# A hash-attention kernel with two gated layers: normalized rows scaled in place before their transposition, and a copy of the queries moved to a DMA

## The chip, the cores and the metric

The kernel runs on one core of one Trainium2 chip. The metric is device time in microseconds (us) of one execution; lower is better. The time of a kernel is the median of its timed runs.

## The reference, cut to what matters

The attention is masked by hash buckets: a query sees a key only where the signs of six projections agree. Its output is normalized row by row (root mean square) and goes through a gated layer and a layer with a squared ReLU. All numbers are float32.

```python
# attention: batch 2, heads 8, seq 768, head_dim 64
q_bits = (np.einsum('bhsd,dk->bhsk', q, proj) > 0)      # and k_bits
q_bucket = np.sum(q_bits * powers, axis=-1)             # and k_bucket
mask = q_bucket[:, :, :, None] == k_bucket[:, :, None, :]
scores = np.where(mask, scale * np.matmul(q, k.transpose(0, 1, 3, 2)), -1e9)
attn = softmax(scores); x = attn @ v                    # -> [1536 tokens, 512]
# first layer, d_ff 1536
rms = np.sqrt(np.mean(x * x, axis=-1, keepdims=True) + 1e-06)
xn = x / rms * rms_g
g = xn @ w_gate; val = xn @ w_val
x = (g * (1.0 / (1.0 + np.exp(-g))) * val) @ w_out
# second layer, d_ff 2048
r = np.maximum(x @ w_in, 0.0)
out = (r * r) @ w_out
```

## The kernel before, in words

The whole program is a list of small operations. Each has a function that issues its instructions, a rank, a cost for each engine that may run it (T is TensorE, D VectorE, A ScalarE, P GpSimd, S SyncE's queue), what it reads and writes (`r`, `w`) and which buffers it makes or uses (`new`, `use`). At build time `Plan.run` walks over this list: again and again it takes the operation that can start first by those costs, lower rank first among equals, and gives it to the engine where it starts first. The engines' instructions stand in that order; on the chip each engine runs its own in order, and semaphores hold what isn't ready. A change of one cost, one reader or one engine can so move everything that is planned after it.

**Attention.** There are 16 heads, in two batches of 8, with 6 row tiles each: 96 slots. To keep float32 precision, operands are split into a high and a low part. For each head `plan_prep` loads keys (`rk`) and queries (`rq`), splits the keys into `k1` (high part, twice) and `k2` (low part), and the queries into `q1` (high part in partitions 0 to 63, low part in 64 to 127). `copy_q` writes the high part of the queries a second time, into `q2[0:64]`, from `rq`; the hash bits come into the rows of `q2` below (`hash_pe`, `hash_bits`), and 12 rows of them go by a DMA from ScalarE's queue into `k2` (`hash_dma`). The scores of a slot (`st_S`) are matmuls of `q1` with `k1` and of `q2` with `k2`. `k1`, `k2`, `q1` and `q2` have three buffers each, so a new head's copies wait for the last scores of the head three before.

A slot then goes through `st_min` (VectorE, out of PSUM, with the row maximum), `st_exp` (ScalarE), the split of the probabilities into halves of 16 bits, their transposition and the product with the values (`st_PV`). Slots of one kind transpose on TensorE (`st_TP`, L592, 128x128 transposes by an identity); the others split on ScalarE and GpSimd into `hla`, and SyncE's queue issues a DMA transpose into `Ta` (`st_T`, L585). The same queue issues the loads of the values and of all layer weights (`wraw`, L937). At a head's end `st_evac` scales the result into `xall`, which holds 6 tiles of 128 tokens x 512: the 768 tokens of one batch.

**Norm.** When the eight heads of a batch are done, `plan_norm` runs for each half of `xall` (3 tiles, 384 tokens), so four times in all. ScalarE squares and sums each tile (L834), GpSimd takes a power, VectorE improves it by four Newton steps on 128x3 elements (L851 to L859), which gives `rr`, one factor for each row. `scales` makes three diagonal matrices `diag` of 128x128, identity times `rr`. `x_pe` transposes and scales at once: for each of 4 column blocks, three float32 matmuls of an `xall` block with `diag`. `x_hi` and `x_lo` split the result, times `rms_g`, into the operands `xT` of the layers.

**Layers.** Weights arrive as float64 and are turned into two float32 parts by VectorE and ScalarE (L950 to L979). Products of the first batch's tokens are put in between the second batch's attention; the second batch's follow.

Of the kernel before, what the change touches and what calls it, by code (L numbers as in the profile page):

```python
# [10 lines left out]
F32 = mybir.dt.float32  # L11
# [5 lines left out]
AF = mybir.ActivationFunctionType  # L17
ALU = mybir.AluOpType
# [3 lines left out]
B, H, S, D = 2, 8, 768, 64  # L22
# [8 lines left out]
TT = TB // 128  # L31
# [19 lines left out]
OPS = {'k1': 3, 'q1': 3, 'k2': 3, 'q2': 3}  # L51
# [15 lines left out]
R_QC = -12.8  # L67
# [5 lines left out]
R_S = -4.0  # L73
# [11 lines left out]
R_X = 41.4  # L85
# [16 lines left out]
H_K = 2.7  # L102
# [3 lines left out]
KQ = 'A'  # L106
WQ = 'S'
VQ = 'S'


class Op:
# [130 lines left out]
def tile_hash_attention_moe(  # L242
# [44 lines left out]
    rr = const.tile([128, QT], F32, name="rr")  # L287
    rt = const.tile([128, QT], F32, name="rt")
    idle = const.tile([128, 512], F16, name="idle")
    diag = const.tile([128, TT, 128], F32, name="diag")  # L290

    plan = Plan(dict(
        OPS, **RING, rk=RAW, rq=RAW, vr=2, vl=3, O=1, mo=3, mt=MB[0], mu=MB[1], y=YB, yL=YL,
# [5 lines left out]
    def f32(x):  # L299
        return x.bitcast(F32)  # L300

    def copy(eng, out_, in_):
        if eng == "A":
            nc.scalar.copy(out_, in_)  # L304
        elif eng == "D":
            nc.vector.tensor_copy(out_, in_)
        else:
            nc.gpsimd.tensor_scalar(  # L308
                out=out_, in0=in_, scalar1=1.0, scalar2=0.0, op0=ALU.mult, op1=ALU.add
            )  # L310
# [13 lines left out]
    def dma(name, cost):  # L324

        return {"dma": cost, name: 0.475 if name == "S" else 0.1}
# [53 lines left out]
    def tile_of(h, name, n=3, dtype=F32R):  # L380
        t = heads[h][name] = ap.tile([128, S], dtype, tag=name, name=name, bufs=n)
        return t
# [21 lines left out]
        sub(eng, d["q1"][64:128, c], d["rq"][0:64, c], f32(d["q1"][0:64, c]))  # L404

    def copy_q(eng, h):
        copy(eng, tile_of(h, "q2", OPS["q2"])[0:64], heads[h]["rq"][0:64])

    def s_ring(n):

        return "Sb" if n % 2 and n < XEND else "Sa"
# [126 lines left out]
    def st_S(eng, i):  # L538
        h, t = divmod(i, QT)
        d = heads[h]  # L540
        sp = tiles[i]["sp"] = scores(s_ring(i))
        for n, (a, b2, kr) in enumerate((("q1", "k1", 128), ("q2", "k2", RQ + 2 * NB))):
            for hf in range(2):
                nc.tensor.matmul(  # L544
                    sp[:, hf, 0:TB],
                    d[a][0:kr, t * 128:(t + 1) * 128],
                    d[b2][0:kr, hf * TB:(hf + 1) * TB],
                    start=(n == 0), stop=(n == 1),
                )
# [101 lines left out]
    def plan_prep(h):  # L651
# [14 lines left out]
            D=(0.47, H_K), A=0.733, P=0.8,  # L666
        )
        add(
            lambda e: copy_q(e, h), s0 + R_QC, use=[("rq", h)], new=[("q2", ("q2", h))],
            D=(0.47, H_K), A=0.733, P=0.8,  # L670
        )
        for n, c in enumerate((slice(0, TB), slice(TB, S)) if h == 0 else (slice(0, S),)):
            f = 0.55 if h == 0 else 1.0
# [73 lines left out]
    def plan_slot(i):  # L747
# [2 lines left out]
        space = ["more"] if c == "x" else []  # L750
        ko = [(x, h) for x in ("k1", "q1", "k2", "q2")]
        add(
            lambda e: st_S(e, i), i + R_S, use=ko, r=[("head", h)] + [("bits", 0, 1, 0)] * (h == 0 and t >= TT), new=[(s_ring(i), ("S", i))],
            chain="S", T=0.72, w=[("S", i)],
        )
        if i < W1:
# [103 lines left out]

    def scales(eng, hf, t):

        nc.vector.tensor_scalar(
            out=diag[:, t, :], in0=ident, scalar1=rr[:, hf * TT + t:hf * TT + t + 1],
            scalar2=None, op0=ALU.mult,
        )

    def x_pe(eng, st, blk, c):

        pt = st["p"] = mo()[:, 0:TB]  # L870
        for t in range(TT):
            nc.tensor.matmul(
                pt[:, t * 128:(t + 1) * 128],
                xall[:, blk % 2 * TT + t, c * 128:(c + 1) * 128], diag[:, t, :],
                start=True, stop=True,
            )

    def x_hi(eng, st, blk, c):
# [8 lines left out]
    def plan_norm(blk):  # L887
        hf = blk % 2
        for t in range(TT):
            b = ("junk x", blk, t)  # L890
            add(
                lambda e, t=t: squares(e, hf * TT + t), R_X, r=[("x", hf)], w=[("ss", hf, t)],
                new=[("wv", b)], A=0.65,
            )
        sq = [("ss", hf, t) for t in range(TT)]
        add(lambda e: power(e, hf, 0), R_X, r=sq, w=sq + [("rr", hf)], D=0.07)
        add(lambda e: power(e, hf, 1), R_X, r=sq, w=[("rr", hf)], P=0.9)
        for n in range(4):
            add(lambda e, n=n: newton(e, hf, n), R_X, r=[("rr", hf)], w=[("rr", hf)], D=0.08)
        for t in range(TT):  # L900
            add(
                lambda e, t=t: scales(e, hf, t), R_X, r=[("rr", hf), "ident"], w=[("diag", t)],
                D=0.2,
            )
        tag, p = xt_place[1, blk]
        for c in range(4):
            st, b = {}, ("xp", blk, c)
            add(
                lambda e, st=st, c=c: x_pe(e, st, blk, c), R_X + c, new=[("mo", b)], T=0.65,
                r=[("x", hf)] + [("diag", t) for t in range(TT)],  # L910
            )
            add(
                lambda e, st=st, c=c: x_hi(e, st, blk, c), R_X + c, r=[p, b] + [("xt", blk)] * (c > 0),
                use=[b], new=[("xT" + tag, ("xT", 1, blk))] * (c == 0), A=0.464,
                w=[("xh", 1, blk, c)] + [("xt", blk)] * (c == 0),
            )
            add(
                lambda e, st=st, c=c: x_lo(e, st, blk, c), R_X + c, r=[("xh", 1, blk, c)],
                use=[b, ("xT", 1, blk)], w=[("xT", 1, blk, c)], D=0.53,
            )  # L920
# [408 lines left out]
```

## Time and profile before

| | |
|---|---|
| median of 3 runs | 845.27 us (840.51 to 851.2) |
| the profiled execution | 842.59 us, span 840.8 us |
| PE (TensorE matmul) busy | 789.9 us, 94% of the span |
| DVE (VectorE) busy | 711.3 us, 85% |
| ACT (ScalarE) busy | 460.6 us, 55% |
| POOL (GpSimd) busy | 235.2 us, 28% |

The profile is one execution. The span is the time from the first to the last instruction; the execution's own time is 1.8 us longer. PE counts matmuls and PEld the loads of their stationary operand. SPq and ACTq are the queues in which SyncE and ScalarE issue DMAs. A float32 matmul is recorded as two matmuls, a transpose as one.

### The profile page before, as it was taken

What the parts mean: (1) busy time and instruction counts of PE and PEld (TensorE: products, weight loads), DVE (VectorE), ACT (ScalarE), POOL (GpSimd) and SP (SyncE); (2) the same over time, 40 slices, a digit from 0 to 9 for tenths busy, and PEclk for the clock granted to TensorE, in tenths of its full rate; (3) what the DMA queues carried; (4) which work ended last, traced back from release to release, by engine and by line L of the source; (5) the groups of instructions that cost most, each with busy time, mean ns of one, the idle gap of its engine ahead of it and who ended that gap; (6) DMA issues with size and microseconds to landing.
All of it is one profiled execution on the core that took longest, in us unless ns stands there. A gap on an engine that the chain in (4) does not pass through costs nothing.

```text
span 840.8 us, 14918 instructions
## 1 busy us (share of the span) xinstructions
PE 789.9 (94%) x5633; PEld 718.3 (85%) x5633; DVE 711.3 (85%) x1391; ACT 460.6 (55%) x929; POOL 235.2 (28%) x205
## 2 busy tenths in 40 slices
PE   8989896989879998889899999999999999999998
PEld 4777775889768897889789999999899898998996
DVE  6997888789795998889999999999687787877764
ACT  5888897777777787523355334346552342342320
POOL 7578785656666454000001000000000000000000
PEclk8999998999998999999999999999999999999999
DMA  6465766488976998233334343432320211211003
GB/s 225 124 111 115 150 140 163 99 177 206 194 164 122 193 179 167 79 101 101 101 103 149 101 138 130 133 125 75 104 100 26 76 60 41 101 51 51 26 1 150
DMA packets 126528, 97.74 MB, mean 116 GB/s; under 512 B 106308, under 2 KB 108356, under 8 KB 126456
## 3 DMA queue, kind: packets, MB, share of 16 engines
q1 hardware_dynamic: 122960, 87.97, 40.8%
q10 hardware_dynamic: 3496, 8.81, 3.7%
q8 instruction: 44, 0.72, 0.3%
q14 instruction: 28, 0.23, 0.1%
HBM read 67.12 MB, written 3.15 MB: 84 GB/s over the span
## 4 chain that ended last, share of the span: by engine, by line
PE 67%; DVE 22%; issue 3%; ACT 3%; DMA 3%; POOL 2%; ACTq 0%; SPq 0%; DVEq 0%; POOLq 0%
PE mo L1006 32%; PE mo L1113 16%; PE mo L1102 8%; PE S L544 4%; PE O L618 4%; DVE Pa L555 3%; PE S L423 3%; DMA Ta<-hla 2%; DVE mo L956 2%; DVE acc L1127 2%; DVE mo L966 1%; DVE yl L313 1%; DVE mo L970 1%; DVE mo L961 1%; DVE wil L313 1%
## 5 line engine op out<-in xcount | busy, mean ns | idle before, releaser
L313 POOL TENSOR_TENSOR hla<-Pa,hla 128x768 f16<-128x768 f32 x66 | 110.7, 1678 | 72.1 <-ACT hla L304 64.7
L1127 DVE TENSOR_TENSOR acc<-acc,mo 128x512 f32<-128x512 f32 (+1 forms) x164 | 100.9, 617 | 23.6 <-PE mo L1113 22.9
L544 PE MATMUL S<-k,q 76*128 76x384 f32 (+1 forms) x384 | 91.3, 365 | 11.9 <-DVE Pa L555 7.8
L1032 ACT ACTIVATE mt<-mo 128x384 f32<-128x384 f32 x64 | 31.3, 489 | 101.1 <-PE mo L1006 97.7
L544 PEld LDWEIGHTS S<-k,q 76*128 76x128 f32 (+1 forms) x384 | 66.4, 195 | 19.9 <-DVE Pa L555 9.6
L1113 PE MATMUL mo<-woh,yl 128*128 128x512 f32 x192 | 75.3, 392 | 0.0
L1113 PE MATMUL mo<-wol,yh 128*128 128x512 f32 x192 | 75.2, 392 | 0.0
L1113 PE MATMUL mo<-woh,yh 128*128 128x512 f32 x192 | 74.7, 389 | 0.0
L555 DVE TENSOR_SCALAR_CACHE_REDUCE Pa<-S 128x768 f32<-128x768 f32 x66 | 62.6, 949 | 12.5 <-PE S L544 8.5
L313 DVE TENSOR_TENSOR yl<-mu,yh 128x384 fp32r<-128x384 f32 x112 | 67.7, 612 | 3.8 <-POOL yh L308 2.6
L308 POOL TENSOR_SCALAR yh<-mu 128x384 fp32r<-128x384 f32 x19 | 9.9, 524 | 218.0 <-PE mo L1113 88.1
L308 POOL TENSOR_SCALAR wih<-wv 128x512 fp32r<-128x512 f32 x15 | 9.4, 627 | 215.1 <-ACT mt L1032 109.7
L1036 DVE TENSOR_TENSOR mu<-mt 128x384 f32<-128x384 f32 x64 | 35.3, 552 | 36.1 <-ACT mt L1032 36.0
L1102 PE MATMUL mo<-yh,woh 128*128 128x384 f32 x192 | 65.1, 339 | 0.5 <-DVE wil L313 0.5
L1102 PE MATMUL mo<-yh,wol 128*128 128x384 f32 x192 | 64.5, 336 | 0.1
L1102 PE MATMUL mo<-yl,woh 128*128 128x384 f32 x192 | 64.4, 335 | 0.0
L573 ACT ACTIVATE Pa<-Pa,b 128x768 f32<-128x768 f32 x66 | 62.1, 943 | 3.2 <-ACT b L564 0.3
L1006 PE MATMUL mo<-xTAh,wih 128*128 128x384 f32 x160 | 55.8, 349 | 5.2 <-DVE acc L1127 2.9
L950 ACT ACTIVATE wv<-wraw 128x512 f32<-128x512 f32 x70 | 46.4, 670 | 25.9 <-DMA wraw<-in_w 25.8
L304 ACT CAST hla<-Pa 128x768 f16<-128x768 f32 x66 | 54.8, 833 | 5.6 <-DVE q L432 2.4
L1006 PE MATMUL mo<-xTAh,wil 128*128 128x384 f32 x160 | 55.1, 345 | 1.2 <-DVE wil L313 1.1
L1006 PE MATMUL mo<-xTBh,wih 128*128 128x384 f32 x160 | 54.3, 339 | 1.2 <-DVE mu L1026 1.2
(166 smaller groups left out, 2350.3 us busy)
## 6 DMA issues: line engine op xcount, KB each, us to landing
wraw<-in_w SPq DMA_DIRECT2D x104, 512.0 KB
rk<-in_k ACTq DMA_DIRECT2D x14, 384.0 KB
vr<-in_v SPq DMA_DIRECT2D x8, 384.0 KB
out<-acc SPq DMA_DIRECT2D x12, 256.0 KB
rq<-in_q ACTq DMA_DIRECT2D x14, 192.0 KB
Ta<-hla SPq DMA_TRANSPOSE x66
rk<-in_k SPq DMA_DIRECT2D x2, 384.0 KB
k<-q ACTq DMA_DIRECT2D x15, 36.0 KB
```

Source lines behind the costliest of these rows:

```text
L304: nc.scalar.copy(out_, in_)
L313: engine[eng].tensor_tensor(out=out_, in0=in0, in1=in1, op=ALU.subtract)
L544: nc.tensor.matmul(sp[:, hf, 0:TB], d[a][0:kr, t * 128:(t + 1) * 128], d[b2][0:kr, hf * TB:(hf + 1) * TB], start=(n == 0), stop=(n == 1),)
L555: nc.vector.tensor_scalar(out=e["P"].rearrange("p (a b) -> p a b", a=2), in0=e["sp"][:, :, 0:TB], scalar1=-1e9 / SCALE, scalar2=None, op0= ...
L573: nc.scalar.activation(e["P"], e["P"], AF.Exp, bias=e["b"], scale=SCALE)
L618: nc.tensor.matmul(d["O"][:, t, 0:w], T[:, a, :], b2[:, c, :], start=(c == 0 and n == 0), stop=(c == QT - 1 and n == 2),)
L950: nc.scalar.activation(t, f32(wst[m]["hi"]), AF.Abs)
L1006: nc.tensor.matmul(ps, a[:, c * 128:(c + 1) * 128], b2[:, c, :], start=(c == 0 and n == 0), stop=(c == 3 and n == 2),)
L1036: nc.vector.tensor_tensor(out=us["u"], in0=st["t"], in1=st["t"], op=ALU.mult)
L1102: nc.tensor.matmul(po, a[:, dc * 128:(dc + 1) * 128], b2, start=(j == 0 and n == 0), stop=(j == len(fs) - 1 and n == 2),)
L1113: nc.tensor.matmul(po, a[:, tt * 128:(tt + 1) * 128], b2, start=(j == 0 and n == 0), stop=(j == len(fs) - 1 and n == 2),)
L1127: nc.vector.tensor_tensor(out=ac, in0=ac, in1=st["p"], op=ALU.add)
```

## The change

`scales` no longer writes diagonal matrices: it multiplies each tile of `xall` in place by its rows' factors, 128x512 elements, on ScalarE or VectorE, whichever the plan finds free first. `x_pe` transposes the scaled tile by the identity, with the instruction that `st_TP` uses; the 128x3x128 buffer `diag` is gone. For all heads but the first, `copy_q` becomes a DMA in SyncE's queue that copies `q1[0:64]` to `q2[0:64]`, so it follows the split of `q1` and no longer reads `rq`; the scores of a head wait for it by a token `qc`. The planner's costs are changed to match.

```diff
+QQ = 'S'
...
-    diag = const.tile([128, TT, 128], F32, name="diag")
...
     def copy_q(eng, h):
-        copy(eng, tile_of(h, "q2", OPS["q2"])[0:64], heads[h]["rq"][0:64])
+        t = tile_of(h, "q2", OPS["q2"])
+        if h == 0:
+            copy(eng, t[0:64], heads[h]["rq"][0:64])
+        else:
+            engine[eng].dma_start(out=f32(t[0:64]), in_=f32(heads[h]["q1"][0:64]))
...
         add(
-            lambda e: copy_q(e, h), s0 + R_QC, use=[("rq", h)], new=[("q2", ("q2", h))],
-            D=(0.47, H_K), A=0.733, P=0.8,
+            lambda e: copy_q(e, h), s0 + R_QC, use=[("rq" if h == 0 else "q1", h)],
+            new=[("q2", ("q2", h))], w=[("qc", h)],
+            **(dict(D=(0.47, H_K), A=0.733, P=0.8) if h == 0 else dma(QQ, 0.6)),
         )
...
-            lambda e: st_S(e, i), i + R_S, use=ko, r=[("head", h)] + [("bits", 0, 1, 0)] * (h == 0 and t >= TT), new=[(s_ring(i), ("S", i))],
+            lambda e: st_S(e, i), i + R_S, use=ko, r=[("head", h), ("qc", h)] + [("bits", 0, 1, 0)] * (h == 0 and t >= TT), new=[(s_ring(i), ("S", i))],
...
     def scales(eng, hf, t):
 
-        nc.vector.tensor_scalar(
-            out=diag[:, t, :], in0=ident, scalar1=rr[:, hf * TT + t:hf * TT + t + 1],
-            scalar2=None, op0=ALU.mult,
-        )
+        t += hf * TT
+        if eng == "A":
+            nc.scalar.activation(xall[:, t, :], xall[:, t, :], AF.Copy, scale=rr[:, t:t + 1])
+        else:
+            nc.vector.tensor_scalar(
+                out=xall[:, t, :], in0=xall[:, t, :], scalar1=rr[:, t:t + 1], scalar2=None,
+                op0=ALU.mult,
+            )
...
         for t in range(TT):
-            nc.tensor.matmul(
+            nc.tensor.transpose(
                 pt[:, t * 128:(t + 1) * 128],
-                xall[:, blk % 2 * TT + t, c * 128:(c + 1) * 128], diag[:, t, :],
-                start=True, stop=True,
+                xall[:, blk % 2 * TT + t, c * 128:(c + 1) * 128], ident,
             )
...
             add(
-                lambda e, t=t: scales(e, hf, t), R_X, r=[("rr", hf), "ident"], w=[("diag", t)],
-                D=0.2,
+                lambda e, t=t: scales(e, hf, t), R_X, r=[("rr", hf)], w=[("xn", hf, t)] + [("x", hf)] * (t == 0),
+                A=0.52, D=0.34, port=True,
             )
...
-                lambda e, st=st, c=c: x_pe(e, st, blk, c), R_X + c, new=[("mo", b)], T=0.65,
-                r=[("x", hf)] + [("diag", t) for t in range(TT)],
+                lambda e, st=st, c=c: x_pe(e, st, blk, c), R_X + c, new=[("mo", b)], T=0.34,
+                r=["ident", ("x", hf)] + [("xn", hf, t) for t in range(TT)],
```

## Rows read from the trace of the kernel before

**Rows 1.** Four stages: from:to, length, busy PE PEld DVE ACT POOL, clock, DMA share, GB/s
```profile
0.00:140.00 140.00, 123.77 (x1355) 98.54 (x1355) 117.97 (x259) 115.10 (x254) 100.59 (x93) 0.96 0.61 143
140.00:330.00 190.00, 170.56 (x1578) 152.72 (x1579) 163.49 (x306) 145.91 (x287) 113.98 (x80) 0.96 0.79 166
330.00:438.00 108.00, 96.60 (x590) 92.46 (x589) 98.75 (x197) 46.35 (x97) 5.51 (x8) 0.98 0.33 100
438.00:840.00 402.00, 399.00 (x2110) 374.59 (x2110) 331.10 (x631) 153.19 (x294) 15.11 (x26) 1.00 0.26 88
```

**Rows 2.** The page's chain that ended last, by engine
```profile
PE 67%; DVE 22%; issue 3%; ACT 3%; DMA 3%; POOL 2%; ACTq 0%; SPq 0%; DVEq 0%; POOLq 0%
```

**Rows 3.** The chain at the norms: start us, us, what
```profile
156.17 0.69 DVE diag L863 x3
...
339.88 2.68 PE mo L872 x24
...
347.78 1.35 PE mo L872 x12
```

**Rows 4.** The timeline at the first and third norm: start, us, engine, line, operation
```profile
145.57 4.33 PE L872 MATMUL mo<-diag,xall 128*128 128x128 f32 x24 [3.94 <-DVE diag L863]
...
336.80 0.67 DVE L863 TENSOR_SCALAR diag<-ident,rr 128x128 f32<-128x128 f32 x3
...
339.71 2.84 PE L872 MATMUL mo<-diag,xall 128*128 128x128 f32 x24
```

**Rows 5.** The chain in the attention: transposes on TensorE, at L592
```profile
48.86 0.69 PE mo L592 x6
```

**Rows 6.** Operations nearest to the new scaling, by line: ns min/median/max
```profile
L863 DVE TENSOR_SCALAR diag<-ident,rr x12: 274/278/287, 145.2 to 346.6; 128x128 f32<-128x128 f32 x12
...
L956 DVE TENSOR_SCALAR wv<-wv x70: 406/420/890, 24.1 to 813.0; 128x512 f32<-128x512 f32 x70
...
L834 ACT ACTIVATE wv<-xall x12: 619/641/662, 138.0 to 341.5; 128x512 f32<-128x512 f32 x12
```

**Rows 7.** Copies and splits of the queries into q1 and q2, by line and engine
```profile
L308 POOL TENSOR_SCALAR q<-rq x17: 825/829/1002, 6.7 to 263.8; 64x768 fp32r<-64x768 f32 x17
L304 ACT CAST q<-rq x15: 814/832/838, 6.6 to 264.9; 64x768 fp32r<-64x768 f32 x15
```

**Rows 8.** The chain where a copy of the queries or a head's hash lies on it
```profile
28.18 0.81 POOL q L308
...
116.19 0.84 ACT q L304
...
181.37 2.19 PE S L423 x8
```

**Rows 9.** The timeline at the prep of the twelfth head
```profile
161.50 0.83 POOL L308 TENSOR_SCALAR q<-rq 64x768 fp32r<-64x768 f32 x1 [1.41 <-PE S L544]
```

**Rows 10.** ScalarE's DMA queue over the whole span: packets, MB, share of 16 engines
```profile
q10 hardware_dynamic: 3496, 8.81, 3.7%
```

**Rows 11.** Issues in SyncE's queue by line: ns min/median/max
```profile
L585 SPq DMA_TRANSPOSE Ta<-hla x66: 1273/1444/3123, 38.5 to 331.3; - x66
...
L388 SPq DMA_DIRECT2D rq<-in_q x2: 471/539/607, 1.6 to 9.2; - x2
```

**Rows 12.** Who waited for whom: total us, times, longest
```profile
SPq L585 <- POOL hla L313: 87.6, 35, 6.8
...
POOL q L308 <- PE S L544: 7.2, 5, 2.1
...
PEld L618 <- DMA Ta<-hla: 5.9, 6, 2.0
```

**Rows 13.** The granted clock in two stretches: columns as in the first group
```profile
64.00:141.00 77.00, 67.84 (x869) 56.81 (x868) 65.87 (x145) 67.13 (x155) 58.90 (x52) 1.00 0.63 136
141.70:148.50 6.80, 2.93 (x13) 2.93 (x14) 5.08 (x14) 4.19 (x13) 4.72 (x3) 0.50 1.08 225
```

**Rows 14.** The chain's longest wait for a DMA transpose
```profile
220.66 7.23 DMA Ta<-hla
```

## The prediction, made before the change was run

> **What bounds the kernel now.** I read the busy time by stage first, then the chain of work that ended last, then the norms and the queries' copies where that chain meets them. Four stages differ [rows 1]. From 438 us to the end TensorE is busy 399.0 of 402 us: nothing outside it counts there, and neither part of the change is in that stretch, so those 402 us stay. The gain or loss must come out of the first 438 us, where TensorE idles 16.2, 19.4 and 11.4 us in the three stages, 47 us in all. There no engine is alone: in the attention VectorE runs at 84 to 86%, ScalarE at 77 to 82%, DMA at 0.61 to 0.79 of its time; from 330 to 438 us VectorE is at 91% and ScalarE and GpSimd have room. The chain [rows 2] says the same: 67% TensorE, 22% VectorE, 3% each for ScalarE and DMA, 2% GpSimd. The last 402 us alone are some 48 of TensorE's 67 points. What is left in the first 438 us, of 840.8 us, is 160 us of TensorE, 185 us of VectorE, and some 25 us each of ScalarE and DMA. So a microsecond of TensorE's taken away there is on the chain about one time in three, one of VectorE's two times in five, and one of ScalarE's or GpSimd's one time in twenty.
>
> **Transposes for matmuls.** Each of the four norms issues 12 float32 matmuls, 24 records, which took 2.84 us at the third norm and 4.33 us at the first [rows 4]. The nearest row of what replaces them is the attention's own transposes: 6 in 0.69 us of the chain [rows 5], 0.115 us each, one record. 12 of them are 1.4 us, half the third norm's time. TensorE is thus spared some 1.4 us at each of three norms and 2.1 us at the first: 6.3 us of its 789.9. On the chain lie 24 records of the third norm and 12 of the fourth, 4.03 us [rows 3]; 18 transposes take 2.07 us. Gain there: 2.0 us. At the first norm TensorE had waited 3.94 us for `diag` [rows 4], and the chain passes beside its matmuls; of the 2.1 us I count 0.5. Bounds of the whole: 0 and 6.3 us.
>
> [...]
>
> **Scaling in place for diagonals.** Removed: three VectorE operations of 0.278 us, 0.68 us a norm [rows 4, 6]. Added: three of 128x512. [...] On ScalarE the nearest is the square of the same tile, 0.64 us [rows 6], 1.9 us a norm. [...] At the third it is covered: `diag` was complete at 337.5 us, TensorE came to it at 339.7 us [rows 4]. Only at the second do the diagonals stand on the chain [rows 3]. I take +0.8 us there, and 0.4 to 4.8 us as bounds over four norms: the new wait is TensorE's for the last tile, with whatever the plan puts behind the transposes, and behind the scaling on ScalarE stand the evacuation and the squares of the other half, so a late factor now holds these too. If ScalarE takes the last two norms' scaling, as its free time after 330 us suggests [rows 1], VectorE, which is the chain there, does 1.3 us less; I take -0.7 us, bounds -1.3 and +0.8.
>
> **The queries' second copy.** 15 copies of 64x768 leave ScalarE and GpSimd, at 0.83 us each [rows 7]: 12.4 us of engine time. The chain shows just two of the 30 copies that `q1` and `q2` need, 0.81 and 0.84 us [rows 8], and doesn't tell which of the two is which. I take -1.6 us; bounds 0 and -12.4, the latter if every copy on GpSimd, which the slots' low parts wait behind, were a delay to its end.
>
> What takes their place: 15 DMAs of 197 KB. ScalarE's queue moved 8.81 MB in 3.7% of 840.8 us of all 16 engines [rows 10], 283 GB/s, so one is 0.69 us of DMA time and all are 10.4 us, into stages whose DMA share is 0.61 to 0.79 [rows 1]. By the chain's share of DMA, 25 of 438 us, that is +0.6 us. SyncE's queue issues each in some 0.54 us [rows 11], 8 us in all, and that queue is 0% of the chain [rows 2]. Its new wait is for the split of `q1`. Behind it stand DMA transposes and the weights' loads, and TensorE's product with the values waits for the former. The copy itself has time: the twelfth head's queries were copied at 161.5 us [rows 9] and its hash came to TensorE at 181.4 us [rows 8]; scores follow still later. Bounds: 0 where every transfer is hidden (a gain is excluded: nothing is taken from these queues), and at the other end the second rival's 23 us.
>
> **The sum.** -2.0 - 0.5 + 0.8 - 0.7 - 1.6 + 0.6 = -3.4 us. The profiled execution is 842.6 us, 1.8 us over its span, so 839.2 us; the median shown is 2.7 us above that execution, which gives 841.9 us. Between the two I forecast 840 us, 0.6% less. A measurement of this kernel tells about 2%, 17 us, from no change: below 828 us is faster, above 862 us slower. Since the plan is dealt anew from the second head on, I give this case 834 to 847 us, a chance of 0.60.
>
> **Rivals.**
> 1. The engines' time pays in full. ScalarE's and GpSimd's 12.4 us and TensorE's 6.3 us are all saved, since a list that takes what can start first fills the holes: 842.6 - 18.7 = 824 us, 833 with half of it. For it: the attention stages have no engine under 60% [rows 1], and SyncE's transposes waited 87.6 us for GpSimd's low parts [rows 12]. Against: ScalarE and GpSimd are 5 points of the chain. Chance 0.16.
> 2. SyncE's queue becomes the place that waits. A copy stands at the queue's head until `q1` is split, which itself waits for the last scores of three heads before; the longest such wait was 2.1 us [rows 12]. With the issue of 0.54 us and 0.69 us of transfer, the transposes behind come 3.3 us late. Transposes run from 38.5 us on [rows 11], so the ten copies after the fifth count: 33 us if each delay reached TensorE, 12 us if a third did, which is 855 us; with two thirds, 23 us, it is 866 us. It decides from the point where a transpose's data is ready before the copy's; the chain already has one wait of 7.2 us for a transpose [rows 14]. Against: TensorE's loads waited for transposes 5.9 us in all of 66 [rows 12]. This ends slower than before. Chance 0.13.
> 3. The clock falls at the norms. The stretch from 141.7 to 148.5 us at 0.50 [rows 13] made the first norm's matmuls 1.5 us longer than the third's. One such stretch of 6.8 us costs at most 3.4 us of work; at three further norms up to 10 us: 840 + 3 to 10 = 843 to 850 us. [...] Chance 0.06.
> 4. The change doesn't reach the end: the copies and the scaling are hidden both before and after, TensorE's holes grow by what its work shrinks, 842 to 846 us. Chance 0.05.
>
> **How the numbers follow.** The range is to leave out no more than 2 in 10. Below it lies the lower part of rival 1, above it the upper part of rival 2, and a remainder near both ends of the first case: 828 to 853 us. Faster by over 2% is about half of rival 1, 0.09. Slower by over 2% is a part of rival 2, 0.05. The rest, 0.86, is no change that can be told.
>
> **What the profile after would show.** L872's place should hold 48 transposes instead of 96 records, some 1.4 us for 12 of them at full clock; no VectorE operation writes `diag`; `xall` has 12 more writers of 0.4 or 0.65 us. ScalarE and GpSimd should have 15 fewer copies of 64x768, SyncE's queue 15 more issues. TensorE should be saturated again from some point on, 2 to 6 us earlier; its busy time there must be the same 399 us. The prediction is wrong if that point moves by over 10 us: earlier by fewer waits of GpSimd's and TensorE's in the attention (rival 1), or later with TensorE's waits for transposes well above 6 us (rival 2) or further stretches at clock 0.50 around the norms (rival 3).

## The result, and the profile after

The changed kernel takes 851.6 us, the median of 20 runs (846.51 to 857.48); the kernel before takes 844.9 us, the median of 20 runs on the same chips. The ratio is 1.0085, with a 95% interval of 1.0067 to 1.0102: 0.85% or 7.2 us slower (the two medians differ by 6.7 us), where 0.6% faster was forecast. The time lies inside the range given and on the other side of no change.

The profiled execution after has a span of 849.0 us, before 840.8 us. The four stages after, with the columns of [rows 1]:

```profile
0.00:140.00 140.00, 124.45 (x1351) 99.08 (x1351) 113.73 (x247) 110.70 (x249) 96.43 (x86) 0.95 0.72 162
140.00:330.00 190.00, 171.30 (x1494) 153.29 (x1495) 163.39 (x301) 134.39 (x262) 107.75 (x83) 0.93 0.75 161
330.00:438.00 108.00, 92.31 (x595) 88.35 (x594) 97.98 (x190) 53.60 (x112) 13.24 (x12) 0.95 0.38 106
438.00:840.00 402.00, 400.85 (x2127) 376.93 (x2126) 335.88 (x644) 156.48 (x300) 15.07 (x26) 1.00 0.26 85
```

The last 402 us are full, as before (399.0 us): the loss lies ahead of 438 us. The second stage is the striking one. TensorE is busy as long as before, 171.3 against 170.6 us, and issues 84 matmuls fewer, 24 of them by the transpositions; the granted clock there is 0.93 and not 0.96. So busy time alone hides the loss. I therefore read busy time times granted clock, which is about what TensorE got done, in us at the clock of 1.00: a transposition took 0.115 us there [rows 5] and 0.23 us at 0.50 (below). The clock's column has two digits, so each product holds to about 1 us. First before, then after, in three stretches:

```profile
161.00:241.00 80.00, 73.51 (x642) 65.92 (x641) 69.55 (x120) 62.39 (x122) 51.69 (x37) 1.00 0.83 179
241.00:330.00 89.00, 81.82 (x791) 73.13 (x790) 76.65 (x147) 69.33 (x136) 50.03 (x33) 0.96 0.80 163
330.00:441.00 111.00, 99.55 (x607) 95.41 (x607) 101.68 (x202) 47.74 (x100) 5.51 (x8) 0.98 0.34 105
```

```profile
161.00:241.00 80.00, 66.56 (x516) 58.67 (x517) 68.98 (x121) 53.89 (x111) 45.39 (x36) 0.87 0.73 164
241.00:330.00 89.00, 87.28 (x829) 80.37 (x829) 79.90 (x147) 64.67 (x122) 49.07 (x37) 1.00 0.81 175
330.00:441.00 111.00, 95.31 (x611) 91.16 (x610) 100.98 (x196) 55.14 (x115) 13.24 (x12) 0.95 0.38 107
```

From 161 to 241 us before does 73.5 x 1.00 = 73.5 us of work and after 66.6 x 0.87 = 57.9: it falls back by 15.6 us in the 80 us that follow the first norm, some 7 of them by idle time and the rest by the lower clock. From 241 to 330 us it wins back 8.7 (87.3 against 78.5), and from 330 to 441 us it loses 7.1 (90.5 against 97.6). That is 14.0 us behind; its own work is some 6 us smaller, by 96 records of 0.118 us [rows 4] for 48 of 0.115 us [rows 5], and the span is 8.2 us longer. Up to 441 us as a whole TensorE idles just 2.8 us more than before; the larger part of what it falls behind is the lower clock (0.94 for 0.97). First before, then after:

```profile
0.00:441.00 441.00, 393.87 (x3540) 346.67 (x3541) 383.14 (x766) 308.75 (x638) 220.09 (x179) 0.97 0.62 144
```

```profile
0.00:441.00 441.00, 391.06 (x3454) 343.53 (x3455) 378.10 (x742) 300.23 (x624) 217.43 (x180) 0.94 0.65 148
```

The change did what it says. After, by line: 48 transpositions for 96 records [rows 3], the scaling on ScalarE eight times and on VectorE four, ns min/median/max:

```profile
L881 PE MATMUL mo<-ident,xall x48: 272/419/477, 144.9 to 362.1; 128*128 128x128 f32 x48
...
L870 ACT ACTIVATE xall<-xall,rr x8: 707/723/733, 144.1 to 359.4; 128x512 f32<-128x512 f32 x8
...
L872 DVE TENSOR_SCALAR xall<-xall,rr x4: 478/487/1739, 145.3 to 359.2; 128x512 f32<-128x512 f32 x4
```

The scaling is dearer than its nearest rows [rows 6]: 0.723 us on ScalarE (0.641 there) and 0.487 on VectorE (0.420), with one of 1.74. Most transpositions of the first two norms ran at the lower clock: it was granted at 0.50 from 144.7 to 151.5 and from 178.9 to 182.3 us. The chain after shows them there (start us, us, what):

```profile
147.07 1.12 PE mo L881 x4
...
149.17 1.33 PE mo L881 x6
...
178.80 2.57 PE mo L881 x11
```

The last is 0.23 us for each; twelve at that pace are 2.8 us, no less than the 24 records that they replace [rows 4]. What TensorE and its loads waited for (total us, times, longest) answers to [rows 12]; the first row is L544 and L555 of before, where it was 7.8 us in 10 waits:

```profile
PE S L548 <- DVE Pa L559: 12.5, 12, 2.8
...
PEld L622 <- DMA Ta<-hla: 3.7, 8, 1.5
```

The waits for the DMA transposes have become fewer, 3.7 for 5.9 us. Those for the row maxima `Pa`, which free the scores' buffers, have grown. TensorE's longest single wait in this kernel is another one, in the stretch that loses 7.1 us:

```profile
411.53 0.69 PE L1014 MATMUL mo<-xTAh,wih 128*128 128x384 f32 x1 [6.08 <-DVE wol L313]
```

VectorE converts weights almost without a gap from 405.6 us on, and TensorE stands until it is through. The same wait, 6.0 to 6.1 us, is in every profile with the changed kernel's order or nearly that (e4, e12, e13, e16 and e17 below). In the other orders TensorE waits at most 4.7 us at a time between 330 and 441 us, in the kernel before 2.9.

### The profile page after: what moved, and what is told of

It reads as the page before. It is cut to its first block, busy times and chain, and to the rows that moved or that the text cites. A ratio compares the mean times of both kernels' runs of the same rounds, so it can differ in the third digit from the quotient of the medians.

```text
span 849.0 us, 14861 instructions
## 1 busy us (share of the span) xinstructions
PE 794.1 (94%) x5585; PEld 721.6 (85%) x5585; DVE 714.2 (84%) x1383; ACT 455.2 (54%) x921; POOL 232.5 (27%) x206
## 4 chain that ended last, share of the span: by engine, by line
PE 72%; DVE 18%; ACT 3%; issue 2%; DMA 2%; POOL 1%; SPq 0%; ACTq 0%; DVEq 0%; POOLq 0%
PE mo L1014 33%; PE mo L1121 16%; PE mo L1110 9%; PE S L548 6%; PE O L622 4%; PE S L427 2%; DMA Ta<-hla 2%; DVE Pa L559 2%; DVE mo L974 1%; PE mo L596 1%; DVE mo L964 1%; DVE yl L313 1%; DVE q L436 1%; POOL hla L313 1%; DVE acc L1135 1%
## 5 line engine op out<-in xcount | busy, mean ns | idle before, releaser
L548 PE MATMUL S<-k,q 76*128 76x384 f32 (+1 forms) x384 | 96.5, 378 | 16.2 <-DVE Pa L559 12.5
L548 PEld LDWEIGHTS S<-k,q 76*128 76x128 f32 (+1 forms) x384 | 68.7, 202 | 24.1 <-DVE Pa L559 15.6
L308 POOL TENSOR_SCALAR yh<-mu 128x384 fp32r<-128x384 f32 x24 | 13.1, 546 | 216.8 <-PE mo L1121 88.1
L313 DVE TENSOR_TENSOR yl<-mu,yh 128x384 fp32r<-128x384 f32 x112 | 65.7, 595 | 6.1 <-POOL yh L308 3.2
L308 POOL TENSOR_SCALAR wih<-wv 128x512 fp32r<-128x512 f32 x12 | 7.5, 624 | 208.1 <-ACT mt L1040 109.7
L1014 PE MATMUL mo<-xTAl,wih 128*128 128x384 f32 x160 | 55.9, 349 | 0.0
```

Source lines behind the costliest of these rows:

```text
L313: engine[eng].tensor_tensor(out=out_, in0=in0, in1=in1, op=ALU.subtract)
L548: nc.tensor.matmul(sp[:, hf, 0:TB], d[a][0:kr, t * 128:(t + 1) * 128], d[b2][0:kr, hf * TB:(hf + 1) * TB], start=(n == 0), stop=(n == 1),)
L1014: nc.tensor.matmul(ps, a[:, c * 128:(c + 1) * 128], b2[:, c, :], start=(c == 0 and n == 0), stop=(c == 3 and n == 2),)
```

## The experiments

Three theories stand in what was expected. A: the plan deals a new order, and this order loses time on TensorE, by holes and by the low clock that follows them. B: the norm's new instructions cost it, the transpositions by holding the clock down. C: the copies in SyncE's queue cost it. All ratios are to the kernel before, run on the same chip; 0.1% is 0.84 us. A new deal also moves operations from engine to engine: the kernel before has 1391 instructions on VectorE, 929 on ScalarE and 205 on GpSimd; in e10, which changes two planning numbers and nothing else, they are 1396, 920 and 209. "Order" stands here for both, and no run takes the two apart.

**The two parts alone, each planned for itself.** e1 has the new norm and the copies of before; e2 has the norm of before and the copies by DMA.

```diff
# e1, on the changed kernel
-            engine[eng].dma_start(out=f32(t[0:64]), in_=f32(heads[h]["q1"][0:64]))
+        copy(eng, tile_of(h, "q2", OPS["q2"])[0:64], heads[h]["rq"][0:64])
# e2, on the kernel before
-        copy(eng, tile_of(h, "q2", OPS["q2"])[0:64], heads[h]["rq"][0:64])
+            engine[eng].dma_start(out=f32(t[0:64]), in_=f32(heads[h]["q1"][0:64]))
```

> Only the norm is changed (scaling in place, transposes); the second copy of the queries stays on the engines; the plan is dealt anew. Theory A (the new order of the plan loses the time, by holes on TensorE and the half clock that follows them): anything from 838 to 856 us, with the time going up by about half of the added microseconds at half clock plus the added idle time of TensorE. Theory B (transposes at the norms hold the clock down): near the changed kernel, 849 to 853 us, with half clock at each norm. Theory C (SyncE's queue and the copies' DMAs cost the time): below the kernel before, 838 to 843 us.

> Only the queries' second copy is changed (a DMA in SyncE's queue); norm with diagonals as before; the plan is dealt anew. Theory A: anything from 838 to 856 us, again told by TensorE's holes and half clock. Theory B: as the kernel before or a little less, 842 to 845 us. Theory C: 850 to 855 us, with TensorE waiting longer for DMA transposes.

e1: 846.1 us, ratio 1.0009 (0.9984 to 1.0034). e2: 839.05 us, 0.9941 (0.9914 to 0.9968), faster than both kernels. One part does nothing, the other gains 0.6%, together they lose 0.85%: the parts don't add, so what each does in an order of its own doesn't explain the whole. C as a cost of the queue by itself falls: with all 15 DMAs in the queue e2 is the fastest kernel of this study.

**The change in the order of before.** In e3 the list of operations with its costs, readers and engines is that of before, so every engine's order stays; only what `scales`, `x_pe` and the copies issue is new. The scaling falls to VectorE, and a head's DMA is issued right behind the split of `q1`. e5 is e3 with ordinary matmuls by the identity, e6 is the norm's half of e3, e7 the copies' half. In e3, e5 and e7 `copy_q` copies for the first head alone.

```diff
# e3; e6: the first two hunks; e7: the third; e5: all, with matmul for transpose
-            out=diag[:, t, :], in0=ident, scalar1=rr[:, hf * TT + t:hf * TT + t + 1],
+            out=xall[:, hf * TT + t, :], in0=xall[:, hf * TT + t, :],
+            scalar1=rr[:, hf * TT + t:hf * TT + t + 1], scalar2=None, op0=ALU.mult,
...
-            nc.tensor.matmul(
+            nc.tensor.transpose(
-                xall[:, blk % 2 * TT + t, c * 128:(c + 1) * 128], diag[:, t, :],
+                xall[:, blk % 2 * TT + t, c * 128:(c + 1) * 128], ident,
...
+        if h > 0:
+            nc.sync.dma_start(
+                out=f32(tile_of(h, "q2", OPS["q2"])[0:64]), in_=f32(heads[h]["q1"][0:64])
+            )
```

> Both parts of the change, but planned with the costs, readers and writers of the kernel before, so that every engine has the order of before: scaling in place on VectorE at the diagonals' places, transposes at the matmuls' places, and the copy's DMA issued right behind the split of q1. Theory A: faster than before, 838 to 843 us, half clock as before (27 us) or less. Theory B: slower than before, 848 us or more, half clock at the norms. Theory C: slower than before, 849 us or more, with TensorE waiting for transposes over 10 us.

> The third experiment (both parts in the order of the kernel before) with ordinary matmuls by the identity in place of the norms' transposes. There the half clock that begins at 141.4 us lasted 17.1 us, in the kernel before 6.8 us, with the same waits ahead of it. Theory B (transposes don't lift the clock again, matmuls do): half clock at the first norm of about 7 us as before, and 842 to 845 us although TensorE has more to do. Rival (something else in the new instructions holds the clock or the time, scaling in place or the copies' DMAs): half clock of 10 us or more there again, and 848 to 851 us.

> Only the norm's part (scaling in place on VectorE, transposes), in the order of the kernel before. Theory B: the whole loss of the third experiment, 846 to 848 us, with some 17 us of half clock from the first norm on. If the copies' DMAs cost it (theory C): 840 to 843 us.

> Only the queries' second copy by DMA, in the order of the kernel before. Theory B: 842 to 844 us, half clock as before. Theory C: 846 to 849 us, with longer waits for DMA transposes.

e3: 847.47 us, 1.0036 (1.0010 to 1.0062). e5: 848.5 us, 1.0058 (1.0026 to 1.0090). e6: 849.05 us, 1.0058 (1.0035 to 1.0080). e7: 845.8 us, 1.0013 (0.9988 to 1.0039). At a fixed order the change costs 0.36%, 3.0 us. Step by step from e7 over e5 to e3 that is +0.13% for the copies, +0.45% for the scaling in place, -0.22% for transpositions instead of matmuls; each difference is uncertain by some 0.4%, so only the sum and the norm's half (e6) are clearly above 0. A had expected e3 to be faster than before, B at 848 us or more; it came out between. e5 speaks against B's transpositions: with matmuls in their place nothing is gained. C finds no support here either, since e7 is level with before within its noise.

Part of what the norm's half loses shows in the chain of e6 at the third and fourth norm (start us, us, what), where that of before had no operation on `diag` at all between 328 and 362 us:

```profile
342.65 1.18 DVE xall L862 x3
...
352.74 1.19 DVE xall L862 x3
```

The scaling stands on the path, twice 1.2 us, on the engine that was busiest there [rows 1]. That is 2.4 of some 4.9 us; where the rest arises isn't shown.

**The new order with other instructions.** e4 keeps the changed kernel's order and has matmuls by the identity. e8 keeps its instructions and gives the plan costs nearer to the measured ones.

```diff
# e4
-            nc.tensor.transpose(
+            nc.tensor.matmul(
+                start=True, stop=True,
# e8
-                A=0.52, D=0.34, port=True,
+                A=0.62, D=0.42, port=True,
...
-                lambda e, st=st, c=c: x_pe(e, st, blk, c), R_X + c, new=[("mo", b)], T=0.34,
+                lambda e, st=st, c=c: x_pe(e, st, blk, c), R_X + c, new=[("mo", b)], T=0.37,
```

> The changed kernel in its own order, with ordinary matmuls by the identity at the norms' transposes (two records each again, the same result up to rounding). Theory A: as slow as the changed kernel or slower by TensorE's 2 to 6 us, 852 to 858 us. Theory B: the clock stays up at the norms, 844 to 848 us. Theory C: 852 us or a little more.

> The changed kernel, planned with the measured costs of its scaling and its transposes (0.62 and 0.42 us for 0.52 and 0.34; 0.37 for 0.34), so the same instructions in yet another order. Theory A (the order is the larger part of the loss): a time that differs from the changed kernel's by 3 us or more, either way. If the instructions alone set the time: 850 to 853 us.

e4: 854.4 us, 1.0112 (1.0077 to 1.0146): without a transposition at any norm it is no faster, against B. e8: 855.36 us, 1.0126 (1.0091 to 1.0162): costs nearer to the measured ones gave no better order; that it is worse than the changed kernel's is at the edge of the noise (0.41%, uncertain by 0.4%).

**Other orders of the kernel before, and both kernels profiled again.** e9 and e10 change planning numbers only, no operation.

```diff
# e9
-                lambda e, st=st, c=c: x_pe(e, st, blk, c), R_X + c, new=[("mo", b)], T=0.65,
+                lambda e, st=st, c=c: x_pe(e, st, blk, c), R_X + c, new=[("mo", b)], T=0.7,
# e10, at all three copies of the operands
-            D=(0.47, H_K), A=0.733, P=0.8,
+            D=(0.47, H_K), A=0.75, P=0.82,
```

> The kernel before with one planning number changed: the cost of a norm's transposition group stands at 0.70 instead of 0.65, so that not one instruction differs but the written order does from the first norm on. Theory A (the order of the plan moves the time by about as much as the change did): the ratio is off 1 by 0.3 to 1.2%, that is 2.5 to 10 us either way, without any transposition or scaled tile; the granted clock's low stretches lie elsewhere than in the kernel before and their sum goes with the time, at about half a us for each us. Theory B (only the transpositions or the scaling in place cost): ratio 1.000, within 0.2%.

> The kernel before with two planning numbers of the copies changed (ScalarE 0.75 instead of 0.733, GpSimd 0.82 instead of 0.80), a second other order of the same instructions, now from the first head on. Theory A: off 1 by 0.3 to 1.2%, not by the same amount as the other order, and of the two orders at least one is slower by 0.3% or more. Theory B: 1.000, within 0.2%.

> The kernel before, unchanged, for a second profiled execution. Theory A needs the low stretches of the granted clock to be a property of the order: they should come at the same places as in the first profile (about 12, 60, 142, 254 and 370 us), 27 us in all, within 7 us. The rival is that they come by chance from one execution to the next: other places, another sum; then the 51 against 27 us of the two kernels would show nothing by itself.

> The changed kernel, unchanged, for a second profiled execution. Theory A: low stretches where its first profile has them (12, 77, 114, 145, 165, 179, 199, 220, 360, 408 us), 51 us in all, within 7 us, four of them between 160 and 230 us. The rival (chance): other places and another sum, near that of the kernel before.

e9: 845.16 us, 0.9998 (0.9973 to 1.0024). e10: 853.39 us, 1.0101 (1.0069 to 1.0133). e10 settles that order is enough: the instructions of before, dealt anew by a change of 2% in a cost, lose about as much as the change does. e9 came out as B expected. These are the mean clocks of before again (e11), after again (e12), e9 and e10, each over its span:

```profile
core 0: 838.8 us, clock 0.984
```

```profile
core 0: 851.2 us, clock 0.968
```

```profile
core 0: 843.5 us, clock 0.972
```

```profile
core 0: 855.8 us, clock 0.972
```

The first profiles had 0.984 (before) and 0.969 (after). Read in steps of 0.5 us, the granted clock in the first profile of before is 1.00 in 1619 steps, 0.50 in 51, and between the two only in the 10 at the ends of its five low stretches. At 0.984 it stood at the lower level for 0.016 x 838.8 / 0.5 = 27 us, at 0.968 for 54 us; the first profiles give 27 and 53 us. The places came back in part: of before's five stretches those at 12 and 142 us did, those at 60, 254 and 370 us did not, and in their stead there were some at 181, 328 and 352 us. That the sums agree so closely is luck. The mean clock of every run is on record, and for the kernel before it lay between 0.968 and 0.988 in 115 runs, which is 20 to 54 us at the lower level, 35 in the mean; the shortest of them, 836.9 us, had 0.988, and one of the longest, 850.0 us, had 0.968. The changed kernel spent 44 to 79 us there in 20 runs, 54 in the mean. So chance moves the sum from run to run, and the programs still differ in its mean.

In the mean of their runs e2 has 38 us, e7, e9 and e10 41 each, e14 44, e1 and e15 46, e5 47, e3 49, e6 52, e13 53, e8 and e16 55, e17 57, e4 61. Over 288 runs, each set against the mean of its own kernel, a span is longer by some 0.32 us for each further us at the lower level: my estimate, from a line fitted through these runs, where A had put half a us. By it the changed kernel's 18 us more go with 5.9 of its 7.2 us, and e10's 6 us more with 1.9 of its 8.5. So the changed kernel loses mostly where the clock is lower, and e10 mostly without that: e9 has the same 41 us and is level with before. This tells what goes together, not which is the cause; a hole on TensorE costs time itself, and the changed kernel's stretches at 0.50 from 165.2 and from 407.6 us begin in the holes that end at 165.46 (shown below) and 411.53 us.

**The new order with the old norm, a good order with the new norm, other orders of the change.** e13 takes the changed kernel's order and puts diagonals and matmuls back. e14 takes e2's order and puts the new norm in, by the first two hunks of e3. e15 is the changed kernel with e10's planning numbers; e16 has another cost for the transpositions.

```diff
# e13
-            nc.scalar.activation(xall[:, t, :], xall[:, t, :], AF.Copy, scale=rr[:, t:t + 1])
+            nc.scalar.activation(diag[:, t, :], ident, AF.Copy, scale=rr[:, t:t + 1])
...
-            nc.tensor.transpose(
+            nc.tensor.matmul(
-                xall[:, blk % 2 * TT + t, c * 128:(c + 1) * 128], ident,
+                xall[:, blk % 2 * TT + t, c * 128:(c + 1) * 128], diag[:, blk % 2 * TT + t, :],
+                start=True, stop=True,
# e16
-                lambda e, st=st, c=c: x_pe(e, st, blk, c), R_X + c, new=[("mo", b)], T=0.34,
+                lambda e, st=st, c=c: x_pe(e, st, blk, c), R_X + c, new=[("mo", b)], T=0.40,
```

> The changed kernel's order, engine by engine, but at the norms the instructions of before: three diagonal matrices (on the engine that the new plan gives each scaling to) and float32 matmuls with them; the copies stay DMAs. Theory A (the order): slow all the same, ratio 1.006 to 1.012, 848 to 853 us, with the granted clock low four times between 145 and 230 us as in the changed kernel. Theory B (the norm's new instructions): near before, 0.998 to 1.003. By the prices so far the diagonals save 2.7 us against the scaling in place, and the matmuls cost 1 to 3 us against the transpositions, so that A gives 850 to 853.

> The order of e2_copy_free (copies by DMA, planned for them; 0.994 of before) with the norm's new instructions put in the old ones' places: scaling in place on VectorE and transpositions. If the new norm costs what it did in the order of before (3 us of 845, e6_norm_old_order 5 us): 0.9975 to 1.0000, and then order and norm simply add. Theory A in its strong form (a norm's instructions cost nothing themselves, the order decides): 0.992 to 0.995. Theory B (transpositions start a fall of the clock wherever they stand): 1.003 or more.

> The changed kernel with two planning numbers of the key copies and the first query copy changed (ScalarE 0.75 instead of 0.733, GpSimd 0.82 instead of 0.80), as in e10_before_order3, so the same instructions in another order. Theory A: off the changed kernel's 1.0085 by 0.3% or more, either way. Theory B (the norm's instructions cost, whatever the order): within 0.2% of 1.0085.

> The changed kernel with the planned cost of a transposition group at 0.40 instead of 0.34: the order is the changed kernel's up to the first norm and differs behind it in a tenth as many places as e15_after_order2. Theory A: the loss of the first norm, which lies ahead of most of the differences, stays, so 1.005 to 1.011. Theory B: 1.0085 within 0.2%, so this run speaks only if it comes out below 1.005 or above 1.011.

e13: 851.79 us, 1.0078 (1.0045 to 1.0111). With the norm of before in it, the changed kernel's order is as slow as the changed kernel: A, and against B. e15: 844.44 us, 0.9990 (0.9962 to 1.0018): the changed kernel's own instructions, in another order, are level with before. e16: 850.14 us, 1.0079 (1.0048 to 1.0111), which tells nothing apart, as was said ahead of it. e14: 842.46 us, 0.9974 (0.9945 to 1.0003): against e2's 0.9941 the new norm costs 0.33% there, some 2.8 us (uncertain by 0.4%), about what it cost in the order of before. TensorE's waits for the norm have grown, first e2, then e14 (total us, times, longest):

```profile
PE mo L878 <- DVE diag L869: 3.0, 3, 1.6
```

```profile
PE mo L877 <- DVE xall L868: 6.5, 5, 1.8
```

The stretch from 161 to 241 us sorts these kernels by their order. Here it is for e13, then e9, e10 and e15:

```profile
161.00:241.00 80.00, 68.24 (x517) 60.43 (x516) 61.76 (x117) 51.36 (x102) 43.44 (x33) 0.83 0.73 159
```

```profile
161.00:241.00 80.00, 76.84 (x677) 69.53 (x677) 71.72 (x127) 64.09 (x127) 48.80 (x34) 1.00 0.86 184
```

```profile
161.00:241.00 80.00, 70.77 (x603) 63.42 (x602) 65.82 (x118) 56.91 (x113) 46.15 (x35) 0.94 0.75 168
```

```profile
161.00:241.00 80.00, 68.16 (x590) 58.99 (x589) 59.47 (x116) 58.91 (x118) 48.95 (x33) 0.89 0.79 177
```

In busy time times clock, as above:

| order | kernels, us of work from 161 to 241 us |
|---|---|
| of before | before 73.5, e7 73.0, e5 72.7, e3 71.2, e6 69.6 |
| of the changed kernel | after 57.9, e4 56.6, e13 56.6 |
| nearly that of the changed kernel | e16 57.0, e17 56.6 |
| of e2 | e2 72.4, e14 66.1 |
| others | e9 76.8, e1 74.4, e10 66.5, e8 63.6, e15 60.7 |

Between the first two lines lie 12 to 17 us, whatever stands at the norms; inside the first line 4. The second profiles of before and after, e11 and e12, have 72.4 and 58.5. Part of it is put off and not lost, since the plan deals the matmuls differently over the stretches, as after's gain from 241 to 330 us shows: e15 has 60.7 here and ends level, and of e14 and e10, with 66 each, one is at 0.9974 and the other at 1.0101. The stretch tells the orders apart; it doesn't give their times.

**One hole mended.** In the changed kernel's order TensorE waits 2.83 us before the scores at 165.46 us. First the timeline of its TensorE row and then of VectorE and GpSimd, after:

```profile
165.46 1.65 PE L548 MATMUL S<-k,q 128*128 128x384 f32 x4 [2.83 <-DVE Pa L559]
...
160.95 1.53 DVE L313 TENSOR_TENSOR yl<-mu,yh 128x384 fp32r<-128x384 f32 x1
162.41 2.12 DVE L974 SCALAR_TENSOR_TENSOR wv<-wraw,wv 128x512 uint32<-128x512 uint32 x1
164.45 0.94 DVE L559 TENSOR_SCALAR_CACHE_REDUCE Pa<-S 128x768 f32<-128x768 f32 x1
...
162.15 1.83 POOL L313 TENSOR_TENSOR hla<-Pa,hla 128x768 f16<-128x768 f32 x1
```

VectorE has two operations ahead of the maximum for which TensorE waits, and they take 1.53 and 2.12 us, where such operations have medians of 0.55 and 0.68 us. GpSimd works beside both: the cast ends some 0.6 us after GpSimd's subtraction does. e13 has the same hole at the same place, though its norm is another:

```profile
165.10 1.65 PE L549 MATMUL S<-k,q 128*128 128x384 f32 x4 [2.88 <-DVE Pa L560]
```

e17 puts the two behind the maximum and the next cast behind the next one.

```diff
-        for o in plan.run():
+        order = plan.run()
+        order[852:858] = [order[n] for n in (853, 854, 856, 857, 852, 855)]
+        order[863:866] = [order[n] for n in (864, 865, 863)]
+        for o in order:
```

> The changed kernel with three VectorE operations of one stretch in another place: the low part of a product and a cast of a weight behind the row maximum of slot 55 instead of ahead of it, the next cast behind that of slot 56. Theory A, if this hole is carried to the end: the hole of 2.83 us before the scores at 165 us is gone, with it the low stretch of the clock at 165 us (6.8 us, some 3.4 us of work), so 2 to 6 us less than the changed kernel, ratio to before 1.002 to 1.006. Rival: the plan's next wait takes it up (the cast comes late to the product that is queued behind the scores, which already waits 3.4 us for a weight at 169 us), ratio 1.007 to 1.010, with a longer wait for that weight.

e17: 853.56 us, 1.0103 (1.0055 to 1.0151). The rival had it: the hole moves on by one slot, behind the same cast, which takes 2.15 us there too:

```profile
168.49 1.65 PE L548 MATMUL S<-k,q 128*128 128x384 f32 x4 [2.45 <-DVE Pa L559]
```

So removing this hole alone gains nothing that can be measured. (The wait of 3.4 us for a weight, which the expectation above puts at 169 us, ends at 199.0 us in the changed kernel; the wait that took the hole up is the next maximum's.) The comparison is blurred by the clock: up to 161 us the two programs are alike, yet from 141 to 161 us the granted clock was 0.58 in e17 and 0.83 in after.

## Why the prediction was wrong

**The step that failed** is the sum. It took its terms from the chain of one order and charged them to a program in another, and let the new deal in as a spread of a few us around the sum ("834 to 847"). The deal is worth more than all terms together: relative to before, the operations of before in other orders came to 0.9998 and 1.0101 (e9, e10), those of the change to 0.9990 to 1.0126 (the changed kernel, e8, e15, e16). The changed kernel's order alone, with the norm of before, is 0.78% slow (e13), 6.6 us; from e3 to the changed kernel, the same change in its own order, are 4.1 us (0.49%, uncertain by 0.3%). The sum also had no term for the lower clock, which was left to the third rival, and most of the changed kernel's loss goes with it: 54 us for 35 in the mean of the runs.

**The terms**, measured at the order of before, where they had been read: predicted -3.4 us, measured +3.0 (e3).
- Transpositions: -2.5 predicted; -1.9 (e3 against e5) and, in the new order, -2.3 (after against e4), each uncertain by some 3.4 us. Count and pace were right at the clock of 1.00 (1.47 us for 12 at the changed kernel's third norm); at its first two norms and at the fourth (3.01 us for 12) the clock of 0.50 took the gain back.
- Scaling: +0.8 and -0.7 predicted; +3.8 from e7 to e5, uncertain by some 3.5, on the whole inside the bounds of 0.4 to 4.8 given for the four norms. No run shows the +0.8 itself, which was put at the second norm; in its place the chain of e6 has 1.28 us of scaling there for the 0.69 us of diagonals before [rows 3], 0.6 more. The claim that it is covered at the third norm was wrong: in e6 it lies on the chain at both norms of the second batch, 1.2 us each. The cover was read off TensorE's arrival, but there VectorE is the path. The relief of -0.7 needed ScalarE; in the old order the scaling stays on VectorE, so that term wasn't tried by itself.
- Copies: -1.0 in sum predicted; +1.1 at the old order (e7), within 2.1 us of nothing. In an order of its own the part gained 5 us (e2). I put that down to the order; that the plan made use of the freed time of ScalarE and GpSimd isn't excluded.

**The rivals.** The first (the engines' time pays in full) is out: 12.4 us of ScalarE and GpSimd came free, and at the old order (e7) nothing followed; no run comes near 824 us. The second (SyncE's queue) was the one that I gave most of the slower side, and it isn't what happened: TensorE's waits for the transposes fell, 5.9 us [rows 12] to 3.7, and e2 is fast with the same queue. (A third and two thirds of its 33 us are 11 and 22, not 12 and 23; nothing hangs on that.) The third saw the sign, the place and nearly the size (843 to 850 us): further stretches at the lower clock around and after the norms. That the transpositions bring them, theory B, is not what the runs show: with matmuls in their place the time at the lower level is no shorter, 53 us (e13) and 61 (e4) for the changed kernel's 54, and at the old order 47 (e5) for 49 (e3). That I gave this rival 0.06 and that it came out near the number is partly luck, since it is the order that brings these stretches: e15 has all the new instructions, 46 us there, and is level with before. The fourth (hidden before and after) describes e1 and e15.

**The marks that were named.** 48 transpositions, no `diag`, 15 fewer copies, 15 more issues: all seen. The last stretch is as busy as before (400.85 us for 399.0). TensorE's last product with the values starts at 349.1 us, before at 337.5 us: 11.6 us later, over the 10 us that I had set as the sign of a wrong prediction, and with further low clock, not with longer waits for transposes.

**What stays open.** Why this order is the worse one is only located: TensorE does 15.6 us less from 161 to 241 us, with holes behind row maxima and the lower clock after them, and it waits 6.1 us for VectorE's weights at 411 us, a wait that no run removes. Which decision of the plan makes it so isn't shown, nor whether it is the sequence or the choice of engines; the one hole that I mended moved on. C, in the changed kernel's own order, is argued from the shorter waits for transposes and from e15: no run takes the copies' DMAs out of that order.

## What to carry to other kernels

Where a planner deals the order anew, run a change twice: in the frozen order of before, which gives what its instructions cost (here +0.36%), and with a planning number moved and no instruction changed, which gives what a deal is worth (here up to 1.0%). A term smaller than that is no ground for a forecast of sign; forecast the deal's spread first. Of the eight new deals measured here (e1, e2, e8, e9, e10, e15, e16 and the change itself) one was faster by 0.6%, three were level and four slower by 0.79% or more.
Read TensorE's progress as busy time times granted clock, stretch by stretch: the busy time of the second stage was the same in both kernels while the work done differed by some 5 us, 159 against 164. And read the mean clock of every run: one profile of the kernel before shows 27 us at the lower level, its runs 20 to 54.
A part that only frees an engine may still pay in an order of its own: e2, the copies by DMA alone, is 0.9941 of before and the best version found. That was found by running it, not by its terms.

## What the runs showed of the hardware

- Some of VectorE's operations in SBUF took longer while GpSimd worked. Of the changed kernel's 70 casts at L974 that write `wv`, 63 took 0.67 to 0.69 us; the other seven took 0.85 to 2.12 us, and during each of them GpSimd was at work for over a third of the time. A scaling of 128x512 in place took 1.74 us, with GpSimd at work all the while, against a median of 0.487. Not every operation beside GpSimd was slower: three of the like operations at L978 kept 0.68 to 0.69 us with GpSimd at work beside them for 0.28 to 0.68 us. Why the one is slower and the other not, no row shows.
- The time at the lower clock changes from run to run of one program (20 to 54 us in 115 runs of the kernel before) and in its mean from program to program (35 us before, 54 in the changed kernel). In the kernel before the longer runs had more of it, 45 us in the mean of the longest quarter and 25 in the shortest; between programs it doesn't always rank the times (e9 and e10, 41 us both, 1% apart).
- A transposition of 128x128 float32 took about 0.23 us with the clock at 0.50 (11 in 2.57 us from 178.8 us in the changed kernel), twice the 0.115 us of [rows 5].
